# Projected states for block 0 as well: pairs (0,1), (2,3), (4,5), (6,7) in an attention and two-MLP kernel

## Chip, cores and metric

One Trainium2 (trn2) chip, of which the program uses one core. The metric is the device time of one execution in microseconds (us). All data are float32; the large products run in the engine's fp32r form, with every operand split into a high part and the rest, and three of the four partial products taken (`TERMS`).

## What is computed

For x of shape (8, 8, 512, 64) (batch, head, position, depth) and 32 states per batch and head, both attentions below are taken, the two results are joined along the positions, heads are laid side by side (512 columns), and the 4352 rows go through two MLPs.

```python
scores = scale * np.matmul(x, state.transpose(0, 1, 3, 2))      # softmax over the 32 states
xread = np.matmul(a, state)
scores2 = scale * np.matmul(state, x.transpose(0, 1, 3, 2))     # softmax over the 512 positions
sread = np.matmul(a2, x)
...
h = x @ w_in                                                     # 512 -> 2048, float64 weights in memory
g = np.maximum(h, 0.0) + alpha * np.minimum(h, 0.0)
y = g @ w_out                                                    # 2048 -> 512
...
h2 = y @ w2_in
out = (h2 - np.tanh(h2)) @ w2_out
```

The MLP weights lie in memory as 64-bit numbers; the kernel reads them as pairs of 32-bit words and makes float32 pairs of them itself.

## The kernel before

**Blocks and visits.** A block is one batch of 512 rows; block 8 holds the 256 rows of `sread`. The first MLP goes over the blocks; of each it makes 16 visits (block, f), f being one slice of 128 of the 2048 inner columns. The order of visits is written out: (0, 0..7), (1, 0..15), (0, 8..15), (2, 0..15), (3, ...) and so on. A visit issues, in this order: `emit_h` (L607), the first product into `ps_h`; the plan's "early" work; `act_a` (L621), the leaky slope on ScalarE and VectorE; "gap" and "mid" work; `emit_o` (L635) of the visit two before, 12 matmuls of the second product into four banks; `act_b`, the split of g; then "late" and "end" work and the stores. All engines run their own instructions in program order. What stands in "early", "gap" and so on is a timetable written by hand: `at(i, f, place, work)` from L1017 on. The second MLP follows (Strassen-like chunks and pairs) and is not touched.

**First product.** For blocks 1 to 7 the matrix that multiplies w_in is not `xread` but the attention matrix (two groups of four heads, `X[0, blk, g]`), and w_in is multiplied by the states beforehand: `project_one` (L401) takes three matmuls for quarter q (512 of the 2048 columns), group g and half p, and makes a high and a low part (ScalarE L415, VectorE L416). So h needs 2 x 3 = 6 matmuls. A projection serves two blocks at once: two blocks' states share the 128 columns of the product, and the halves that belong to the other block go through DRAM (`pw_dram`) and are read back by `load_parts` (L429). The pairs are (1,2), (3,4), (5,6), and 7 alone. `SN` holds the split states that a projection reads: `state_mask` (L348) and `state_turn` (L355) make them, with one VectorE operation each (L351, L371).

**Block 0** works otherwise: `spread` (L479) and `read` (L584) make `xread` itself, in four pieces of 128 rows (fp32 matmuls, then a split on ScalarE and VectorE, L338 and L339), and h takes 4 x 3 = 12 matmuls with the plain w_in (L614).

**Conversion of the weights.** 32 jobs, 16 for slices of w_in and 16 for slices of w_out, in the order of `jobs` (L128). A job's words come by one DMA of 512 KB into a ring of four `raw` tiles; then ScalarE takes the absolute value (`conv_a`), VectorE clamps and shifts (`conv_b`, L116 and L118), joins the sign (`conv_s`, L121), ScalarE and GpSimd make the high and low parts (`conv_c`, `conv_d`). A tick (`conv_step`, in two halves) moves every job in flight by one phase: tick t runs `conv_b` and `conv_s` of job t - 2 and `conv_d` of job t - 4, and loads job t + 1. The 36 ticks stand: 6 in the opening, two a visit in (0, 0..7), and 14 in (1, 0..13).

**Opening.** Before the first visit a list written by hand runs the attention of block 0 (`a` for the first four heads, `c` for the other four), with the ticks between its steps:

```python
for z in [a.spread, a.s0, a.s1, tick, a.s2, c.spread, a.s2t, c.s0, a.s3, c.s1, a.s3x, c.s2, c.s2t, c.s3,
          a.s4, c.s3x, tick, a.s4m, a.s4t, c.s4, tick, tick, c.s4m, c.s4t, a.r0, a.r1, tick,
          c.r0, c.r1, slopes, tick, load_next_x, load_next_x]:
    z()
```

**Queues.** Every DMA is issued by SP, in program order: an issue that must wait (a raw tile not yet free, a part not yet made) holds all that come behind it. After its use w_in is written to DRAM for block 8 (`save_w_in`, eight transfers of 1 MB, in (0, 9) to (0, 15) and (2, 1) to (2, 7)); the half sums of block 0's y are stored after (0, 7) and read back in (0, 10).

Of the kernel before, what the change touches and what calls it, by code (L numbers as in the profile page):

```python
# [35 lines left out]
def attention_and_two_mlps(ctx, tc, x, state, w1_in, w1_out, alpha, w2_in, w2_out, out):  # L36
# [32 lines left out]
    mask = const.tile([P, GH], F32, name="mask")  # L69
    par = const.tile([P, 2], F32, name="par")  # L70
# [30 lines left out]
    def raw_words(r, layer, f, half):  # L101
        if half == 0:
            wi = w1_in if layer == 0 else w2_in
            nc.sync.dma_start(
# [3 lines left out]
        else:  # L108
            wo = w1_out if layer == 0 else w2_out
            nc.sync.dma_start(out=r.rearrange("p e w -> p (e w)"), in_=wo[f * P:(f + 1) * P, :])  # L110
# [17 lines left out]
    jobs = [(0, 0)] + [j for f in range(1, NF // 2) for j in ((f, 0), (f - 1, 1))] + [(7, 1)]  # L128
# [216 lines left out]
    def lead(b):  # L345
        return b if b % 2 or b == B - 1 else b - 1
# [26 lines left out]
    def parts_tile(b, q, g):  # L373
        if b == 1 and q < 3:
            open_wo(NF // FQ - 1)
            t = WO[NF // FQ - 1][:, :, 2 * (q % 2) + g, :]
        else:
# [6 lines left out]
               for b in range(1, B) if b == lead(b) for q in range(NF // FQ) for g in range(NG)}  # L384

    def staged(b):


        if b > 1:
            return (work.tile([P, DM], F32R, tag="cm", name="ph", bufs=3),  # L390
                    work.tile([P, DM], F32R, tag="cq", name="pl", bufs=3))
        k = n_staged[0]
        n_staged[0] += 1
        if k < 4:
            open_wi(NF // FQ - 1)
            return tuple(WI[NF // FQ - 1][:, i, k % NCC, :] for i in range(2))
        return tuple(work.tile([P, DM], F32R, tag=t, name="pe", bufs=1) for t in (("e2", "e2t"), ("sc", "at"))[k % 2])

    n_staged = [0]

    def project_one(b, q, g, p):  # L401


        both = b + 1 < B
        cols, d = (slice(2 * p, 2 * p + 2), slice(0, P)) if both else (slice(3 * p, 3 * p + 1), slice(p * HP, (p + 1) * HP))
        ps = ps_a.tile([P, DM], F32, tag="a", name="ps_p")[:P if both else HP]
        for k, (i, j) in enumerate(TERMS):
            nc.tensor.matmul(ps, lhsT=SN[b, g][:, i, cols, :].rearrange("p k m -> p (k m)"),  # L408
                             rhs=WI[q][:, j, g * NP + p, :], start=(k == 0), stop=(k == 2))
        if b == 1 and p == 0:  # L410
            parts_tile(b, q, g)
            hi, lo = PW[b, q, g]
        else:
            hi, lo = staged(b)
        nc.scalar.copy(hi[d], ps)  # L415
        nc.vector.tensor_tensor(lo[d], ps, hi[d].bitcast(F32), op=ALU.subtract)  # L416
        if b == 1:

            e = slice((1 - p) * HP, (2 - p) * HP)
# [32 lines left out]
    def attention(b, g, spare=False):  # L452
# [26 lines left out]
        def spread():  # L479
            sn = work.tile([P, 2, NP, 2, D], F32, tag="sn", name="sn")[:, 0]  # L480
            nc.vector.tensor_tensor(
                sn.rearrange("p a q d -> p (a q) d"),
                SG[b, g].unsqueeze(1).to_broadcast([P, GH, D]),
                mask.unsqueeze(2).to_broadcast([P, GH, D]), op=ALU.mult)
            st["sn"] = sn

        def s0():
            if b == 0:
                ps = psum([P, S], "ps_st")
                for p in range(NP):  # L490
                    nc.tensor.transpose(ps[:, p * P:(p + 1) * P],
                                        st["sn"][:, p].rearrange("p q d -> p (q d)"), ident)
                stt = work.tile([P, NP, HP], F32, tag="stt", name="stt", bufs=4)
                for p in range(NP):
                    nc.scalar.copy(stt[:, p], ps[:, p * P + p * HP:p * P + (p + 1) * HP])
                STT[b, g] = stt
# [87 lines left out]
        def read(p):  # L584
            if b == 0:
                ps = ps_acc.tile([P, S], F32, tag="acc", name="ps_x")
            else:
                ps = psum([P, S], "ps_x")
            nc.tensor.matmul(ps, lhsT=st["sn"][:, p].rearrange("p q d -> p (q d)"), rhs=st["at"],
                             start=True, stop=True)  # L590
            split_x(0, b, g * NP + p, S, ps)

        def s6():
# [8 lines left out]
        steps = dict(spread=spread, s0=s0, s1=s1, s2=s2, s2t=s2t, s2b=s2b, s3=s3, s3x=s3x, s3b=s3b, s4=s4, s4m=s4m,  # L602
                     s4t=s4t, s4b=s4b, s5=s5, s6=s6, r0=partial(read, 0), r1=partial(read, 1))
# [753 lines left out]
```

## Time and profile before

| | |
|---|---|
| median of 3 runs | 1460.18 us (1459.79 to 1461.02) |
| the profiled execution's own time | 1461.7 us |
| its span, first to last instruction | 1459.9 us |
| mean granted TensorE clock | 0.985 of full speed |
| TensorE busy | 1399.3 us, 96% of the span |
| VectorE, ScalarE, GpSimd busy | 67%, 50%, 37% |

The profile is one execution. A page gives the sums of each engine and a strip of 40 equal slices; windows give the same sums for chosen stretches; groups give operations of one line with count, busy time (overlaps counted once) and mean duration; waits say which engine stood idle until which other had finished; the timeline gives instructions in order of time. TensorE is PE, VectorE DVE, ScalarE ACT, GpSimd POOL, SyncE SP there. Since matmuls overlap, the time that one costs is busy time over count and not the mean duration.

### The profile page before, as it was taken

What the parts mean: (1) busy time and instruction counts of PE and PEld (TensorE: products, weight loads), DVE (VectorE), ACT (ScalarE), POOL (GpSimd) and SP (SyncE); (2) the same over time, 40 slices, a digit from 0 to 9 for tenths busy, and PEclk for the clock granted to TensorE, in tenths of its full rate; (3) what the DMA queues carried; (4) which work ended last, traced back from release to release, by engine and by line L of the source; (5) the groups of instructions that cost most, each with busy time, mean ns of one, the idle gap of its engine ahead of it and who ended that gap; (6) DMA issues with size and microseconds to landing.
All of it is one profiled execution on the core that took longest, in us unless ns stands there. A gap on an engine that the chain in (4) does not pass through costs nothing.

```text
span 1459.9 us, 22884 instructions
## 1 busy us (share of the span) xinstructions
PE 1399.3 (96%) x8188; PEld 1190.5 (82%) x8188; DVE 972.6 (67%) x1430; ACT 730.7 (50%) x1322; POOL 538.8 (37%) x414
## 2 busy tenths in 40 slices
PE   5779999999999899999999999999999999999998
PEld 2557677777787777778987888888879999999998
DVE  7889756556767677765446646465357698777874
ACT  4666644444655555654334545454355354444443
POOL 3645400000455455446001221122025576666662
PEclk8989999999999999999999999999999999999999
DMA  6447438976777777679836774543978733444421
GB/s 164 137 140 197 129 136 286 314 248 173 217 209 222 210 241 209 219 232 312 258 102 254 256 251 157 211 176 141 346 263 313 257 105 128 145 138 138 145 81 37
DMA packets 227906, 288.12 MB, mean 197 GB/s; under 512 B 57808, under 2 KB 133584, under 8 KB 226768
## 3 DMA queue, kind: packets, MB, share of 16 engines
q1 hardware_dynamic: 227792, 286.66, 61.4%
q8 instruction: 64, 1.05, 0.3%
q14 instruction: 50, 0.41, 0.1%
HBM read 166.54 MB, written 117.96 MB: 195 GB/s over the span
## 4 chain that ended last, share of the span: by engine, by line
PE 61%; DMA 6%; DVE 6%; ACT 2%; issue 2%; POOL 1%; SPq 1%; ACTq 0%; DVEq 0%; POOLq 0%
PE ps_m L1027 21%; PE ps_m L837 17%; PE acc L645 12%; PE ps_h L617 6%; PE ps_m L911 2%; DMA gt<-g 1%; DMA pw<-pw 1%; DVE g L629 1%; DVE ps_h L624 1%; DMA c_raw<-in_moe_w_in 1%; PE ps_p L408 1%; DMA ch<-wc 1%; DMA g<-t 1%; ACT g L628 1%; DVE c_m L121 1%
## 5 line engine op out<-in xcount | busy, mean ns | idle before, releaser
L645 PE MATMUL acc<-g,wo 128*128 128x512 f32 (+1 forms) x1728 | 405.8, 384 | 2.8 <-ACT g L628 1.4
L645 PEld LDWEIGHTS acc<-g,wo 128*128 128x128 f32 x1728 | 311.8, 190 | 75.0 <-issue 6.5
L1027 PE MATMUL ps_m<-wp,s 128*128 128x256 f32 x2856 | 343.4, 283 | 1.4 <-ACT e L1010 1.4
L1027 PEld LDWEIGHTS ps_m<-wp,s 128*128 128x128 f32 x2856 | 342.9, 192 | 1.9 <-ACT e L1010 1.8
L837 PE MATMUL ps_m<-x,ch 128*128 128x512 f32 x1344 | 306.5, 390 | 2.9 <-ACT c L843 2.2
L837 PEld LDWEIGHTS ps_m<-x,ch 128*128 128x128 f32 x1344 | 251.9, 188 | 57.0 <-ACT c L843 3.4
L972 DVE TENSOR_TENSOR s<-gt,s 128x512 fp32r<-128x512 f32 (+1 forms) x216 | 214.4, 1043 | 46.7 <-ACT s L988 45.7
L629 DVE SCALAR_TENSOR_TENSOR g<-ps_h,sign,g 128x512 fp32r<-128x512 f32 (+1 forms) x144 | 103.5, 719 | 156.2 <-ACT g L628 155.9
L628 ACT ACTIVATE g<-ps_h,sign 128x512 fp32r<-128x512 f32 (+1 forms) x144 | 95.5, 663 | 174.2 <-PE acc L645 120.3
L988 ACT CAST s<-gt 128x512 fp32r<-128x512 f32 (+1 forms) x216 | 120.0, 596 | 80.9 <-PE ps_m L1027 39.0
L617 PE MATMUL ps_h<-x,pw 128*128 128x512 f32 x600 | 157.3, 397 | 3.0 <-DMA pw<-pw 2.4
L624 DVE SCALAR_TENSOR_TENSOR ps_h<-ps_h,sign,t 128x512 f32<-128x512 f32 (+1 forms) x144 | 104.4, 725 | 67.1 <-ACT t L623 66.3
L617 PEld LDWEIGHTS ps_h<-x,pw 128*128 128x128 f32 x600 | 110.0, 188 | 28.6 <-issue 3.2
L238 POOL TENSOR_TENSOR c_q<-c_m,c_q 128x512 int32<-128x512 int32 x32 | 41.3, 1291 | 242.2 <-DVE c_m L121 223.7
L850 POOL TENSOR_TENSOR t<-c,t 128x512 f32<-128x512 f32 x32 | 44.9, 1402 | 230.7 <-ACT t L847 225.8
L623 ACT ACTIVATE t<-ps_h,slope 128x512 f32<-128x512 f32 (+1 forms) x144 | 95.8, 665 | 54.3 <-PE ps_h L617 53.9
L859 DVE TENSOR_TENSOR c<-ps_m,c 128x512 f32<-128x512 f32 x96 | 65.7, 689 | 84.2 <-PE ps_m L837 71.8
L847 ACT ACTIVATE t<-c 128x512 f32<-128x512 f32 x96 | 60.6, 633 | 85.3 <-DVE c L859 73.6
L265 POOL TENSOR_TENSOR c_o<-c_q,c_o 128x512 fp32r<-128x512 f32 (+1 forms) x48 | 55.8, 1163 | 95.4 <-ACT c_o L263 95.4
L954 POOL TENSOR_TENSOR s<-gt,gt 128x512 f32<-128x512 f32 (+1 forms) x36 | 54.7, 1529 | 87.5 <-DMA gt<-g 86.6
L843 ACT COPY c<-ps_m 128x512 f32<-128x512 f32 x96 | 56.0, 586 | 51.1 <-PE ps_m L837 43.6
L168 POOL TENSOR_TENSOR cq<-cm,cq 128x512 int32<-128x512 int32 x32 | 42.5, 1329 | 95.2 <-DVE cm L121 68.4
(142 smaller groups left out, 1657.9 us busy)
## 6 DMA issues: line engine op xcount, KB each, us to landing
g<-t SPq DMA_DIRECT2D x128, 256.0 KB, 2.3
gt<-g SPq DMA_DIRECT2D x64, 512.0 KB, 4.8
wc<-c_o SPq DMA_DIRECT2D x112, 256.0 KB, 3.7
ch<-wc SPq DMA_DIRECT2D x56, 512.0 KB, 6.9
pw<-pw SPq DMA_DIRECT2D x96, 256.0 KB, 5.5
wp<-wc SPq DMA_DIRECT2D x28, 512.0 KB, 7.3
xr<-in_x SPq DMA_DIRECT2D x64, 128.0 KB, 3.1
raw<-in_moe_w_in SPq DMA_DIRECT2D x16, 512.0 KB, 3.9
```

The costliest lines, as they stand in the source:

```text
L617: nc.tensor.matmul(ps[:, :n], lhsT=w[i], rhs=xt[:, j, :n], start=(k == 0 and m == 0), stop=(k == len(pairs) - 1 and m == 2))
L623: nc.scalar.mul(t, ph, slope[:, f:f + 1])
L624: nc.vector.scalar_tensor_tensor(ph, ph, sign[:, f:f + 1], t, op0=ALU.mult, op1=ALU.max)
L628: nc.scalar.mul(g[:, 0, :n], ph, sign[:, f:f + 1])
L629: nc.vector.scalar_tensor_tensor(g[:, 1, :n], ph, sign[:, f:f + 1], g[:, 0, :n].bitcast(F32), op0=ALU.mult, op1=ALU.subtract)
L645: nc.tensor.matmul(acc[t][:, :n], lhsT=w[i][:, t * P:(t + 1) * P], rhs=g[:, j, :n], start=(first and k == 0), stop=(last and k == 2))
L837: nc.tensor.matmul(b, lhsT=w[p][:, cc], rhs=XT[key, i][cc][:, q], start=(i not in GOES_ON and cc == k == 0), stop=(cc == 1 and k == 2), sk ...
L847: nc.scalar.activation(t, h, AF.Tanh)
L859: nc.vector.tensor_tensor(h, ps[j, i], h, op=ALU.add)
L972: nc.vector.tensor_tensor(made[k - 1][:, 1], src, made[k - 1][:, 0].bitcast(F32), op=ALU.subtract)
L988: nc.scalar.copy(made[k][:, 0], source(blk, i, jj))
L1027: nc.tensor.matmul(dst[:, t * HW:(t + 1) * HW], lhsT=s[:, p, r, t * P:(t + 1) * P], rhs=w[:, q], start=first, stop=(jj == NJ // 2 - 1 and ...
```

## The change

Block 0 gets projected states too. The pairs become (0,1), (2,3), (4,5), (6,7), with the even block first; `spread` and `read` go, and h of block 0 takes 6 matmuls. The states of blocks 0 and 1 are masked and turned in the opening. Quarter 0 is projected at the end of the opening, quarter 1 in (0,2) and (0,3), quarters 2 and 3 in (1,4), (1,5), (1,9), (1,10). For quarters 0 and 1 a projection writes both parts to staging tiles, copies block 0's halves by DMA into the tile that h reads, and block 1's to DRAM; for all others everything goes through DRAM, and block 1 reads all its parts by `load_parts`. The jobs are reordered: four slices of w_in come first, (7, 0) is job 8, and w_out's slices 1 to 7 follow. The ticks stand: 8 in the opening, two a visit in (0, 0..3), one in (0, 4..7), 16 in (1, 0..13). Three loads of states and the first load of weights are issued by ScalarE's queue. The half sums are read into two spare `x` tiles instead of `raw` tiles.

```diff
-    jobs = [(0, 0)] + [j for f in range(1, NF // 2) for j in ((f, 0), (f - 1, 1))] + [(7, 1)]
+    jobs = [(0, 0), (1, 0), (2, 0), (3, 0), (4, 0), (0, 1), (5, 0), (6, 0), (7, 0)]
+    jobs += [(f, 1) for f in range(1, 8)]
...
-        raw_words(raws[k], 0, *jobs[k])
+        raw_words(raws[k], 0, *jobs[k], nc.sync if k else nc.scalar)
...
     def lead(b):
-        return b if b % 2 or b == B - 1 else b - 1
+        return b - b % 2
...
-        if b == 1 and q < 3:
+        if (b == 0 and q < 2) or (b == 1 and q < 3):
             open_wo(NF // FQ - 1)
             t = WO[NF // FQ - 1][:, :, 2 * (q % 2) + g, :]
...
+    def staged(b, q, g, p):
+        if b > 0:
             return (work.tile([P, DM], F32R, tag="cm", name="ph", bufs=3),
                     work.tile([P, DM], F32R, tag="cq", name="pl", bufs=3))
+        if q < 2:
             open_wi(NF // FQ - 1)
+            t = WI[NF // FQ - 1][:, :, 2 * g + p, :]
+        else:
+            if len(extra) < 2:
+                extra.append(xpool.tile([P, 2, S], F32R, tag="x", name=f"extra{len(extra)}"))
+            t = extra[p]
+        return t[:, 0], t[:, 1]
...
+        ps = ps_a.tile([P, DM], F32, tag="a", name="ps_p")
         for k, (i, j) in enumerate(TERMS):
+            nc.tensor.matmul(ps, lhsT=SN[b, g][:, i, 2 * p:2 * p + 2, :].rearrange("p k m -> p (k m)"),
                              rhs=WI[q][:, j, g * NP + p, :], start=(k == 0), stop=(k == 2))
+        hi, lo = staged(b, q, g, p)
+        nc.scalar.copy(hi, ps)
+        nc.vector.tensor_tensor(lo, ps, hi.bitcast(F32), op=ALU.subtract)
+        d, e = (slice(k * HP, (k + 1) * HP) for k in (p, 1 - p))
+        if b == 0 and q < 2:
+            if p == 0:
+                parts_tile(b, q, g)
+            for k, t in enumerate((hi, lo)):
+                nc.sync.dma_start(out=PW[b, q, g][k][d].bitcast(F32), in_=t[d].bitcast(F32))
             for k, t in enumerate((hi, lo)):
                 nc.sync.dma_start(out=pw_dram[b, q, g][p, k, e], in_=t[e].bitcast(F32))
             return
         for k, t in enumerate((hi, lo)):
+            nc.sync.dma_start(out=pw_dram[b, q, g][p, k], in_=t.bitcast(F32))
...
-        if 0 < blk < B:
+        if blk < B:
             col = slice(f % FQ * P, (f % FQ + 1) * P)
             pairs = [([PW[blk, f // FQ, g][i][:, col] for i in range(2)], X[0, blk, g]) for g in range(NG)]
...
+        load_state(0, 0)
+        for b, g in ((0, 1), (1, 0), (1, 1)):
+            load_state(b, g, queue=nc.scalar)
         load_next_x()
+        conv_load(0)
         load_next_x()
-        for k in range(4):
+        for k in range(1, 4):
             conv_load(k)
...
+        for z in [masks[0, 0], turned[0, 0], masks[0, 1], a.s0, turned[0, 1], masks[1, 0], masks[1, 1], tick, a.s1, tick,
+                  turned[1, 0], turned[1, 1], a.s2, tick, a.s2t, c.s0, a.s3, tick, c.s1, a.s3x, c.s2, c.s2t, tick, c.s3,
+                  a.s4, c.s3x, a.s4m, tick, a.s4t, c.s4, a.s4b, tick, c.s4m, c.s4t, c.s4b, tick, slopes]:
             z()
+        for g in range(NG):
+            for p in range(NP):
+                project_one(0, 0, g, p)
+        load_next_x()
+        load_next_x()
...
-        for f in (*range(10), 12, 13):
-            if f in (5, 12):
+        for f in range(14):
+            if f in (11, 12):
...
-        turns = [(0, 1, 0, (0, "mid"), (2, "early")), (0, 2, 0, (1, "late"), (2, "gap")),
-                 (0, 1, 1, (3, "mid"), (4, "early")), (0, 2, 1, (3, "late"), (4, "mid"))]
+        turns = [(1, 2, 0, (5, "late"), (7, "late")), (1, 2, 1, (8, "late"), (9, "late"))]
...
+        todo = [(0, q, g) for q in range(1, NF // FQ) for g in range(NG)] + [(2, q, g) for q in range(NF // FQ) for g in range(NG)]
+        todo += [(b, q, g) for b in (4, 6) for g in range(NG) for q in range(NF // FQ)]
+        places = [(0, 2), (0, 3), (1, 4), (1, 5), (1, 9), (1, 10), (1, 14), (1, 15)] + [(0, f) for f in range(8, 14)]
+        places += [(0, 15)] + [(2, f) for f in range(15)]
...
+        at(0, 5, "late", partial(load_parts, 1, 0))
+        at(1, 0, "early", partial(load_parts, 1, 1))
+        at(1, 6, "end", partial(load_parts, 1, 2))
+        at(1, 10, "end", partial(load_parts, 1, 3))
+        at(1, 13, "late", partial(load_parts, 0, 2))
+        at(0, 9, "early", partial(load_parts, 0, 3))
...
-        for f in range(NF // 2):
+        for f in range(NF // 4):
             halves(0, f, "late", "end")
```

## Rows read from the trace of the kernel before

**Rows 1.** Page: span, part 1 (busy us), part 2 (GB/s of 40 slices).

```profile
span 1459.9 us, 22884 instructions
...
PE 1399.3 (96%) x8188; PEld 1190.5 (82%) x8188; DVE 972.6 (67%) x1430; ACT 730.7 (50%) x1322; POOL 538.8 (37%) x414
...
GB/s 164 137 140 197 129 136 286 314 248 173 217 209 222 210 241 209 219 232 312 258 102 254 256 251 157 211 176 141 346 263 313 257 105 128 145 138 138 145 81 37
```

**Rows 2.** Windows A to F: busy us of each engine, clock, DMA share, GB/s.

```profile
0.00:30.80 30.80, 18.64 (x50) 9.02 (x51) 20.61 (x47) 13.84 (x27) 7.37 (x11) 0.83 0.59 159
30.80:108.67 77.87, 57.62 (x350) 42.15 (x349) 66.69 (x121) 49.35 (x97) 42.89 (x32) 0.89 0.51 144
108.67:181.92 73.25, 68.53 (x294) 54.16 (x293) 63.71 (x92) 46.63 (x85) 35.38 (x26) 0.97 0.59 162
181.92:195.57 13.65, 13.65 (x93) 11.02 (x92) 9.64 (x19) 5.55 (x11) 1.29 (x1) 1.00 0.00 1
195.57:253.56 57.99, 57.24 (x287) 45.93 (x286) 30.12 (x55) 24.80 (x43) 0.00 (x0) 1.00 0.73 256
253.56:350.38 96.82, 93.61 (x467) 70.25 (x466) 59.06 (x108) 46.04 (x83) 0.00 (x0) 0.98 0.82 254
```

**Rows 3.** VectorE's groups in stretch B: count, busy us, mean ns of one, idle before.

```profile
L118 DVE TENSOR_SCALAR cm<-cm 128x512 int32<-128x512 int32 x16 | 12.8, 798 | 0.5
L121 DVE SCALAR_TENSOR_TENSOR cm<-raw,cm 128x512 int32<-128x512 int32 x16 | 12.1, 753 | 0.2
L116 DVE TENSOR_SCALAR cm<-cm 128x512 f32<-128x512 f32 x16 | 8.3, 518 | 0.0
...
L351 DVE TENSOR_TENSOR sm<-sg,par 128x128 f32<-128x128 f32 x4 | 3.1, 776 | 0.0
...
L371 DVE TENSOR_TENSOR snp<-ps_st,snp 128x128 fp32r<-128x128 f32 x4 | 1.1, 284 | 1.0 <-ACT snp L370 1.0
```

**Rows 4.** VectorE's groups in stretch C.

```profile
L118 DVE TENSOR_SCALAR cm<-cm 128x512 int32<-128x512 int32 x13 | 16.2, 1249 | 0.4
L116 DVE TENSOR_SCALAR cm<-cm 128x512 f32<-128x512 f32 x13 | 10.9, 837 | 0.0
...
L121 DVE SCALAR_TENSOR_TENSOR cm<-raw,cm 128x512 int32<-128x512 int32 x13 | 9.3, 712 | 0.0
L416 DVE TENSOR_TENSOR wo<-ps_p,wo 128x512 fp32r<-128x512 f32 x4 | 2.7, 676 | 0.0
```

**Rows 5.** TensorE's groups in stretch E.

```profile
L617 PE MATMUL ps_h<-x,wi 128*128 128x512 f32 x84 | 20.5, 393 | 0.8 <-DVE g L629 0.8
L408 PE MATMUL ps_p<-wi,snp 128*128 128x512 f32 x49 | 13.9, 390 | 0.0
```

**Rows 6.** Timeline of stretch A: start us, duration us, engine, line, operation.

```profile
18.11 3.75 PE L589 MATMUL ps_x<-at,sn 128*128 128x512 f32 x4 [4.60 <-DVE at L560]
...
30.36 0.18 DVE L89 TENSOR_TENSOR slope<-alpha_sb,sign 128x16 f32<-128x16 f32 x1
...
30.80 0.69 ACT L623 ACTIVATE t<-ps_h,slope 128x512 f32<-128x512 f32 x1
```

**Rows 7.** Timeline of SP from 80 to 90 us.

```profile
84.00 1.18 SPq L421 DMA_DIRECT2D pw<-wi  x2
85.27 1.19 SPq L424 DMA_DIRECT2D wo<-wi  x2
```

**Rows 8.** DMA issues: KB of one, median us from issue to landing.

```profile
pw<-pw SPq DMA_DIRECT2D x96, 256.0 KB, 5.5
...
wo<-pe SPq DMA_DIRECT2D x4, 128.0 KB, 2.2
```

**Rows 9.** Windows of 5 us with full DMA engines.

```profile
10.00:15.00 5.00, 3.28 (x15) 1.49 (x14) 4.01 (x7) 1.54 (x4) 0.00 (x0) 1.00 1.03 343
275.00:280.00 5.00, 3.10 (x14) 1.92 (x13) 2.03 (x4) 1.51 (x4) 0.00 (x0) 1.00 1.02 265
```

**Rows 10.** Waits of the first 360 us: us in all, times, longest.

```profile
ACT g L628 <- PE acc L645: 58.0, 26, 3.6
...
PE ps_h L617 <- DMA wo<-pe: 1.8, 1, 1.8
```

More of the change, by code (lines that the diff above doesn't have):

```diff
@@ L68, in attention_and_two_mlps @@
     ident = const.tile([P, P], F32, name="ident")
-    mask = const.tile([P, GH], F32, name="mask")
-    par = const.tile([P, 2], F32, name="par")
+    par = const.tile([P, 16], F32, name="par")[:, :2]
     alpha_sb = const.tile([P, NF], F32, name="alpha_sb")
@@ L99, in w_out, with raw_words @@
         return WO[f // FQ][:, part, f % FQ, :]
-    def raw_words(r, layer, f, half):
+    def raw_words(r, layer, f, half, queue=nc.sync):
         if half == 0:
             wi = w1_in if layer == 0 else w2_in
-            nc.sync.dma_start(
+            queue.dma_start(
                 out=r.rearrange("p (c f) w -> p c (f w)", c=NCC),
@@ L109, in raw_words @@
             wo = w1_out if layer == 0 else w2_out
-            nc.sync.dma_start(out=r.rearrange("p e w -> p (e w)"), in_=wo[f * P:(f + 1) * P, :])
+            queue.dma_start(out=r.rearrange("p e w -> p (e w)"), in_=wo[f * P:(f + 1) * P, :])
     def high_abs(m, r):
@@ L309, in attention_and_two_mlps, with load_state @@
     xraw, SG = {}, {}
-    def load_state(b, g, tag="sg"):
+    def load_state(b, g, tag="sg", queue=nc.sync):
         sg = work.tile([P, D], F32, tag=tag, name=f"{tag}{b}_{g}", bufs=4)
-        nc.sync.dma_start(out=sg, in_=state[b, g * GH:(g + 1) * GH].rearrange("h n d -> (h n) d"))
+        queue.dma_start(out=sg, in_=state[b, g * GH:(g + 1) * GH].rearrange("h n d -> (h n) d"))
         SG[(b, g) if tag == "sg" else (b, g, 0)] = sg
     def load_x(b, g):
-        if b < 2:
-            load_state(b, g)
         if b == 0:
@@ L477, in transpose_pair @@
             st["xt", p] = xt
[L479 to L485, printed above, removed]
-        def s0():
[L488 to L496, printed above, removed]
+        def s0():
             transpose_pair(0)
@@ L582, in s5 @@
             st["wide"] = wide
[L584 to L591, printed above, removed]
         def s6():
@@ L612, in emit_h @@
         else:
-            w = [WS[f][:, i] if blk else w_in(f, i) for i in range(2)]
+            w = [WS[f][:, i] for i in range(2)]
             pairs = [([w[i][:, cc, :] for i in range(2)], X[0, blk, cc]) for cc in range(NCC)]
@@ L653, in load_half_sum @@
         for k in range(2):
-            t = work.tile([P, 2, S], F32, tag="raw", name="half", bufs=4)
+            t = extra[k].bitcast(F32)
             nc.sync.dma_start(out=t, in_=y_dram[0][2 * k:2 * k + 2].rearrange("c p n -> p c n"))
```

54 lines of the change are left out of this document (11 added, 43 removed).

## The prediction

> **What bounds the kernel now.** I read the page first. Of a span of 1459.9 us TensorE is busy for 1399.3 us, so all its idle time is some 60 us [rows 1]. The second view is the table of windows, cut where visits around the change begin; a visit is (block, f), and its mark is the ScalarE scaling of its h (act_a). I name the stretches A (start to the first act_a), B (visits (0,0) to (1,0)), C (to (1,13)), D (to (0,8)), E (to (2,0)) and F (to (3,0)) [rows 2]. The reader is to see two regimes. In A, B and C together TensorE is idle for 12.2 + 20.3 + 4.7 = 37 us, and VectorE is busy for 66.7 of 77.9 us in B and 63.7 of 73.25 in C: 130.4 of 151.1, a share of 0.863. There the conversion of the weights, which goes through VectorE, sets the pace. In D, E and F TensorE is idle for 0, 0.8 and 3.2 us: there each matmul taken away shortens the run, and VectorE has about half of its time free. Third, the groups of one engine inside B, C and E give the price of each operation [rows 3 to 5], and the timeline shows how A ends [rows 6].
>
> **The change, part by part.**
>
> Block 0's first product has 12 matmuls a visit now and 6 afterwards: 96 fewer, 48 in visits (0,0) to (0,7) and 48 in (0,8) to (0,15). In E 84 of them take 20.5 us, 0.244 each [rows 5]. The projections stay at 64 calls of 3 matmuls (four pairs in place of three pairs and a single block); only their places change. So the change does take about 23 us from TensorE; the question is how much of it lies where TensorE is the bound.
>
> Stretch A. Out go the two spreads, the mask, and the four reads; the reads' fp32 products for the first group of heads alone span 3.75 us of TensorE [rows 6], and their four splits leave VectorE. In come two splits of the attention matrix, four masks and four turns (two of each were made in B), two more conversion jobs (6 before the first act_a, 4 now), and four projections. A conversion job costs VectorE 0.80 + 0.75 + 0.52 = 2.07 us and a turn 0.28 [rows 3]; the low half of a projection, and a split of the same shape, 0.68 [rows 4]. A spread is 256 wide, between a turn (128) and a split (512), so I take 0.5. A mask shows 0.78 [rows 3]; most of the four run before the scores are there, where VectorE is idle (it is busy for 20.6 of 30.8 us [rows 2]), so between 0 and 3.1 I take 1.1. The list grows by 2 x 2.07 + 4 x 0.68 + 2 x 0.68 + 1.1 + 1.1 = 10.4 and loses 4 x 0.68 + 1.0 = 3.7: 6.7 us net. VectorE was done with the list, slopes last, at about 30.5 [rows 6]; so the last low half is ready at about 37.2.
>
> Then comes SP. Each projection issues four DMAs, two into the tile that the product reads and two to DRAM; two issues of this form took 1.19 us [rows 7]. So four projections hold SP for 9.5 us. The first low half is ready three halves earlier, at 35.2; twelve issues (7.1 us) stand from there to the last one that h needs, which lands some 2.2 us behind its issue [rows 8]: 44.5. With the last matmuls act_a comes at 45.0, 14.2 later than now. Bounds: 40 if SP were never late (37.2 + 2.2 + 0.6), 50 if raw words or projections come late in addition.
>
> In A three state loads and the first weight load move to ScalarE's queue. ScalarE is idle there, and SP is spared four issues of about 0.6 us. I book nothing for it: from 10 to 15 us the DMA engines are full already, at a share of 1.03 and 343 GB/s [rows 9]. The Trainium skill, "DMA: Bandwidth & Descriptors", Issuing engines are not separate DMA queues, says that DMAs from any engine run on the same 16 DMA engines, and that a second issuer saves issue time alone. By that rule the first act_a stays at 45.0; if issue time bounded the start, it would come 2.4 us sooner, at 42.6. No row here has a load issued by ScalarE, so the trace cannot yet decide.
>
> Block 1's x loads (eight issues, 4.8 us of SP) stand behind the projections' DMAs, and weight load 9 behind them, issued at about 51; its words are wanted in visit (0,1), and three jobs' words lie ready before it, which hides that; without them it would cost visit (0,1) some 4 us of landing.
>
> Stretches B and C. In B VectorE loses four jobs (12 instead of 16), 8.3 us, and four masks at 0.78 with four turns at 0.28, 4.2 us [rows 3]; projections are four before and after. 66.7 becomes 54.2. In C it gains two jobs, which cost more there (1.25 + 0.84 + 0.71 = 2.80 [rows 4]), 5.6; it loses four low halves, 2.7, and gains two masks, 1.6. 63.7 becomes 68.2. Together 122.4 us of VectorE work instead of 130.4. At the same busy share, 0.863, that is 141.8 us; TensorE's load falls by some 15 us, so fewer operations wait for it, and I take 0.88: 139.1. Two waits are new. H of (0,4) needs the second quarter's tile, whose last DMA is issued in the middle of (0,3). H of (1,12) needs parts that are stored in (1,10) and loaded behind that, one group of them only when a raw buffer comes free in (1,11); a load of this form lands in 5.5 us [rows 8] against some 4 us of cover. The like wait for a DMA is 1.8 us in the trace [rows 10]. Between 0 and 4 us for both, most of it under VectorE's own work: 1. Act_a of (1,13) comes at 45.0 + 139.1 + 1 = 185.1, where it is at 181.9: +3.2. Bounds for B and C: 131.6 (share 0.93) to 146.
>
> D gets four projections, 12 matmuls at 0.284 (13.9 us for 49 [rows 5]), +3.4; and h of (0,8) loses six, -1.5. D's DMA share is 0.00 now [rows 2], which covers the stores.
>
> E loses 42 matmuls in h, 10.2 us, and two projections, 1.7. But E moves 256 GB/s x 58 us = 14.8 MB now [rows 2]; with one more load of 1 MB and one visit's stores (1 MB) less it is the same in 46 us, 322 GB/s, where slices of the page reach 346 at most [rows 1]. When the engines were full, from 275 to 280, TensorE stood for 1.9 us [rows 9]. So +2, between 0 and +8. F loses two projections, -1.7; block 6 stores twice what block 7 did, 4 MB more in F, where 254 GB/s becomes about 300: booked at 0, up to +4. Behind F the diff leaves the work as it is.
>
> **Sum:** 3.2 + 3.4 - 1.5 - 10.2 - 1.7 + 2.0 - 1.7 = -6.5. The profiled execution took 1461.7 us, 1.5 over the median of the runs, 1460.18. 1461.7 - 6.5 = 1455.2 for an execution like it, 1453.7 for the median.
>
> **Rivals.**
>
> (a) The start is not given back, and the run gets slower. B and C are then set by the waits inside a visit (ScalarE waited 58.0 us for the second product over the first 360 us [rows 10]) and not by VectorE's amount. B falls by its four jobs alone, 8.3, C grows by 5.6 and the new waits by 2: (1,13) comes 14.2 - 8.3 + 5.6 + 2 = 13.5 late, and with D to F (-9.7) the sum is +3.8: 1464. It decides where (1,13) comes over 9.7 late, behind 191.6. For it: in B TensorE (57.6 of 77.9) and VectorE are both well used and neither is full. Against: both lose over 10 us there.
>
> (b) The transfers take E's gain. If spread over visits they go no faster than the present 256 GB/s, E stays near 54 instead of 48: +6 more, 1459.7, no measurable change. For it: the stall at 275 us. Against: D lies empty and takes 2 MB of the stores.
>
> (c) B and C get denser, since TensorE and VectorE are both relieved: at 0.93, 131.6 us, (1,13) comes 4.3 us early, and the sum is -14.0: 1446.2.
>
> **How the numbers follow.** Forecast 0.53 (1449 to 1457), (c) 0.15, (b) 0.17, (a) 0.15. A measurement of this kernel tells about 0.2%, 2.9 us, from no change. Faster is the forecast with (c), 0.68; the same is (b), 0.17; slower is (a), 0.15. The range, 1445 to 1463, leaves out the far parts of (a) and (c), some 0.17 together; it holds the bounds of A (-5 and +5, in part recovered in B) and of the DMA terms.
>
> **What would show it.** In the new profile: first act_a near 45, with SP issuing almost without a gap for 9 us before it and VectorE nearly idle for its last 6; act_a of (1,0) near 107, of (1,13) near 185; D near 15.5 and E near 48, with six h matmuls a visit; a DMA share over 0.9 through E. If the first act_a lies at 40 or 50, the step on SP or that on the raw words fails. If (1,13) comes behind 191, VectorE's amount was not the bound. If E is longer than 52 with TensorE idle, the transfers were under-priced. F shorter by more than 4 us, or the rest behind it moved, would be something that I have not seen.

## The result, and the profile after

The changed kernel is slower: 1468.84 us, median of 4 runs (1467.59 to 1469.69), against 1459.99 for the kernel before beside it (4 runs, 1457.52 to 1461.02). The ratio is 1.0062 [1.0045, 1.008]. The time lies above the whole predicted range.

The page of the changed kernel has the span and the busy times that answer to [rows 1]:

```profile
span 1467.8 us, 22725 instructions
...
PE 1382.1 (94%) x8084; PEld 1176.6 (80%) x8084; DVE 972.0 (66%) x1427; ACT 728.7 (50%) x1320; POOL 535.8 (37%) x414
```

TensorE does 17.2 us less, where the prediction had reckoned about 23, and the span is 7.9 us longer: TensorE now idles for 85.7 us instead of 60.6. The windows of the changed kernel, cut at the same marks as [rows 2] (A to F in order; columns as there), say where:

```profile
0.00:48.90 48.90, 18.10 (x47) 9.55 (x48) 31.51 (x60) 19.27 (x38) 15.23 (x17) 0.73 0.64 164
48.90:114.92 66.02, 49.20 (x304) 34.51 (x304) 52.38 (x97) 41.11 (x76) 31.81 (x24) 0.86 0.67 184
114.92:196.03 81.11, 68.36 (x277) 52.66 (x276) 64.96 (x91) 47.68 (x87) 37.88 (x30) 0.92 0.63 187
196.03:213.23 17.20, 16.64 (x104) 13.23 (x103) 12.63 (x26) 8.05 (x15) 1.29 (x1) 1.00 0.26 94
213.23:263.48 50.25, 47.99 (x241) 36.65 (x240) 30.46 (x59) 23.54 (x42) 0.00 (x0) 1.00 0.92 313
263.48:359.00 95.52, 91.86 (x468) 71.75 (x467) 57.90 (x108) 45.57 (x84) 0.00 (x0) 1.00 0.87 288
```

Length against before: A +18.1, B -11.85, C +7.9, D +3.55, E -7.7, F -1.3, and -0.7 behind F. (One slip of the prediction: its F ends at act_a of (2,15), not of (3,0). The last row here is cut at the same visit, so the difference stands.) The reader is to see two things. E and F did shrink, nearly as forecast. And act_a of (1,13) comes at 196.0, 14.1 late: the start lost 18.1 us and B and C gave back only 4 of them, although VectorE has 13 us less to do there (117.3 instead of 130.4). Its share in B and C fell to (52.38 + 64.96) / 147.13 = 0.80.

The waits of the changed kernel over its first 370 us (us in all, times, longest) name what TensorE now stands for:

```profile
ACT g L594 <- PE acc L611: 64.4, 29, 3.3
...
ACT t L589 <- PE ps_h L583: 39.5, 26, 8.2
...
PE ps_h L583 <- DMA wo<-pw: 6.0, 2, 5.4
PE ps_h L583 <- DMA pw<-pw: 4.7, 2, 3.1
...
PE ps_h L583 <- DMA wo<-wi: 3.7, 1, 3.7
...
PE ps_h L583 <- DMA xs<-xw: 2.0, 1, 2.0
```

L583 is the first product, L589 the changed kernel's act_a, L594 its act_b. Before, the first product waited for a DMA once, for 1.8 us [rows 10]; now four visits wait 16.4 us together. `wo<-wi` is the opening; `xs<-xw` is the wait of (0,4): the product reads the tile in `wo`, and the weight loads beside it wait for `wo<-wi`, so that the small load which the row names seems to have landed at about the same moment; `wo<-pw` is (1,8) and `pw<-pw` is (1,12). The first, from the timeline of the end of stretch A (start us, duration us):

```profile
35.65 2.75 SPq L414 DMA_DIRECT2D wo<-wi  x2
...
38.44 1.24 SPq L416 DMA_DIRECT2D pw<-wi  x2
39.79 1.18 SPq L414 DMA_DIRECT2D wo<-wi  x2
...
44.91 1.19 SPq L414 DMA_DIRECT2D wo<-wi  x2
46.15 1.23 SPq L416 DMA_DIRECT2D pw<-wi  x2
...
47.25 3.33 PE L583 MATMUL ps_h<-x,wo 128*128 128x512 f32 x7 [3.74 <-DMA wo<-wi]
...
47.89 2.39 PEld L583 LDWEIGHTS ps_h<-x,wo 128*128 128x128 f32 x6 [0.17 <-DMA wo<-wi]
48.90 0.69 ACT L589 ACTIVATE t<-ps_h,slope 128x512 f32<-128x512 f32 x1 [8.15 <-PE ps_h L583]
```

SP issues sixteen DMAs from 35.65 to 47.4, each pair into the tile followed by a pair to DRAM that nothing needs for 40 us. The last pair for the tile goes out at 44.91; the product can go on at 47.25, and its last weights (PEld) have landed at 47.89. The longest wait, from the timeline of (1,8):

```profile
147.88 4.18 SPq L426 DMA_DIRECT2D wo<-pw  x4
...
156.23 1.62 PE L583 MATMUL ps_h<-x,wo 128*128 128x512 f32 x3 [5.43 <-DMA wo<-pw]
...
160.02 0.69 ACT L589 ACTIVATE t<-ps_h,slope 128x512 f32<-128x512 f32 x1 [7.19 <-PE ps_h L583]
```

The load of block 1's parts for quarter 2 stands in (1,6) "end", but SP reaches it behind x loads, raw words and stores only at 147.88. The product stands from 150.80 on. The four transfers take 6.7 to 7.4 us each from issue to landing, so that the first two, one group of heads, are there 8.3 us after the first issue and the other two at 158.2.

### The profile page after: what moved, and what is told of

The parts are those of the page before. It is cut to its first block, busy times and chain, and to the rows that moved or that the text cites. A ratio compares the mean times of both kernels' runs of the same rounds, so it can differ in the third digit from the quotient of the medians.

```text
span 1467.8 us, 22725 instructions
## 1 busy us (share of the span) xinstructions
PE 1382.1 (94%) x8084; PEld 1176.6 (80%) x8084; DVE 972.0 (66%) x1427; ACT 728.7 (50%) x1320; POOL 535.8 (37%) x414
## 4 chain that ended last, share of the span: by engine, by line
PE 59%; DMA 7%; DVE 6%; ACT 2%; issue 2%; POOL 1%; SPq 1%; ACTq 0%; DVEq 0%; POOLq 0%
PE ps_m L993 20%; PE ps_m L803 17%; PE acc L611 12%; PE ps_h L583 6%; DMA gt<-g 1%; PE ps_m L877 1%; DMA pw<-pw 1%; DMA wp<-wc 1%; DVE ps_h L590 1%; DVE g L595 1%; PE ps_p L404 1%; DMA ch<-wc 1%; DMA c_raw<-in_moe_w_out 1%; ACT g L594 1%; DMA g<-t 1%
## 5 line engine op out<-in xcount | busy, mean ns | idle before, releaser
L594 ACT ACTIVATE g<-ps_h,sign 128x512 fp32r<-128x512 f32 (+1 forms) x144 | 95.5, 663 | 184.0 <-PE acc L611 129.1
L583 PE MATMUL ps_h<-x,pw 128*128 128x512 f32 x648 | 170.8, 398 | 12.5 <-DMA pw<-pw 8.0
L583 PEld LDWEIGHTS ps_h<-x,pw 128*128 128x128 f32 x648 | 118.7, 189 | 41.0 <-issue 9.8
L589 ACT ACTIVATE t<-ps_h,slope 128x512 f32<-128x512 f32 (+1 forms) x144 | 95.8, 665 | 65.9 <-PE ps_h L583 65.4
L813 ACT ACTIVATE t<-c 128x512 f32<-128x512 f32 x96 | 60.6, 632 | 85.6 <-DVE c L825 77.9
```

The costliest lines, as they stand in the source:

```text
L583: nc.tensor.matmul(ps[:, :n], lhsT=w[i], rhs=xt[:, j, :n], start=(k == 0 and m == 0), stop=(k == len(pairs) - 1 and m == 2))
L589: nc.scalar.mul(t, ph, slope[:, f:f + 1])
L594: nc.scalar.mul(g[:, 0, :n], ph, sign[:, f:f + 1])
L813: nc.scalar.activation(t, h, AF.Tanh)
```

## The experiments

**Theory 1**, formed from that trace: the loss is waits for DMAs, SP's order in A and the loads of parts in C. **Theory 2**: B and C are set neither by these nor by VectorE's amount, but by the rows of waits inside a visit, or by another engine. The first four runs were made on the changed kernel.

**Parts earlier in block 1.** Loads of quarters 2 and 3 split by group and moved up; block 1's double ticks and two x loads moved out of their way.

```diff
-        at(1, 6, "end", partial(load_parts, 1, 2))
-        at(1, 10, "end", partial(load_parts, 1, 3))
+        at(1, 5, "end", partial(load_parts, 1, 2, (0,)))
+        at(1, 6, "gap", partial(load_parts, 1, 2, (1,)))
+        at(1, 10, "early", partial(load_parts, 1, 3, (0,)))
+        at(1, 10, "end", partial(load_parts, 1, 3, (1,)))
...
-            if f in (11, 12):
+            if f in (9, 10):
...
-                    for j, f in (((1, 4), (1, 10)), ((0, 9), (0, 15)))[i] if i < 2 else ((i, 6), (i, 13)):
+                    for j, f in (((1, 7), (1, 13)), ((0, 9), (0, 15)))[i] if i < 2 else ((i, 6), (i, 13)):
```

> Block 1's parts of quarters 2 and 3 are loaded earlier (and the x loads that stand before them on SP later; the two double ticks move from (1,11), (1,12) to (1,9), (1,10), so that the raw tile is free). Theory 1, h of (1,8) and (1,12) waits for DMAs and the time is lost there: the two waits of TensorE, 5.9 and 4.7 us, go to under 1 us each, stretch C falls from 81.1 to about 72 us, and the run from 1468.8 to about 1460. Theory 2, VectorE's conversions set C anyway and the waits lie beside them: C stays within 2 us of 81, the run within 2 us of 1469.

1466.5 us in one run. Windows B and C of this kernel:

```profile
50.07:116.75 66.68, 50.94 (x304) 36.12 (x304) 52.18 (x97) 41.05 (x75) 31.75 (x24) 0.84 0.66 181
116.75:194.06 77.31, 68.47 (x281) 52.47 (x280) 63.21 (x91) 47.80 (x87) 38.13 (x29) 0.93 0.65 192
```

C loses 3.8 us of the 9 that theory 1 hoped for; (1,8) still waits 3.3, and VectorE's share in C is 0.82. Waits for parts remain, so this run does not say what C would be without them. A's opening is unedited here and yet ends at 50.07, 1.2 us later than in the changed kernel: so much do two equal openings differ.

**Tile first.** The opening's DMAs to DRAM are kept back until all that h reads are issued.

```diff
-                nc.sync.dma_start(out=pw_dram[b, q, g][p, k, e], in_=t[e].bitcast(F32))
+                held.append(partial(nc.sync.dma_start, out=pw_dram[b, q, g][p, k, e], in_=t[e].bitcast(F32)))
+            if (g, p) == (NG - 1, NP - 1):
+                while held:
+                    held.pop(0)()
```

> For quarters 0 and 1, SP issues the DMAs into the tile that h reads first and block 1's stores to DRAM behind them. Theory 1, SP's order sets the first h: six issues of 0.61 us fewer stand before it, the first act_a comes at 45.2 instead of 48.9, the wait before (0,4) shrinks from 2.0 to under 1 us, and the run gets 3 to 5 us shorter, 1464 to 1466. Theory 2, the next stretches are set by VectorE's work: the first act_a moves to 45.2, but B grows by as much and the run stays within 1 us of 1469.

1473.27 us in one run. Windows A and B, and a wait of this kernel:

```profile
0.00:45.28 45.28, 18.25 (x47) 10.03 (x48) 31.33 (x60) 19.36 (x39) 15.41 (x17) 0.77 0.62 161
45.28:116.32 71.04, 52.02 (x304) 36.75 (x304) 52.16 (x97) 41.12 (x75) 31.77 (x24) 0.81 0.68 181
```

```profile
ACT cm L110 <- DMA raw<-in_moe_w_out: 5.3, 1, 5.3
```

A shortens by 3.6 us, six issues at some 0.61: SP's order did set the end of A. But B grows by 5.0. The next weight load now stands behind the kept-back stores and x loads, and ScalarE waits 5.3 us for its words, the very "4 us of landing" that the prediction had called hidden. It was hidden only while the start was late. The total fits neither theory: the run is 4.4 us slower than the changed kernel, of which A and B hold 1.4; it is one run.

**Both edits together.**

> Both edits together. Theory 1: the gains add, A 45, B 65, C 72 us, the run at 1456 to 1458, that is 2 to 4 us under the kernel before. Theory 2: the run stays at 1466 to 1469.

1465.61 us (5 runs, 1464.08 to 1466.47), ratio 1.0040 [1.0024, 1.0057]. Windows B and C; A ends at 45.19:

```profile
45.19:114.05 68.86, 49.31 (x304) 34.51 (x304) 52.07 (x97) 41.13 (x76) 31.67 (x24) 0.88 0.69 186
114.05:193.95 79.90, 69.54 (x281) 53.10 (x280) 63.37 (x92) 47.73 (x87) 38.20 (x29) 0.91 0.64 186
```

The gains of A and C do not add up; the wait for raw words is still 4.4 us.

**All loads of the start issued by SP again.**

```diff
-        raw_words(raws[k], 0, *jobs[k], nc.sync if k else nc.scalar)
+        raw_words(raws[k], 0, *jobs[k])
...
-            load_state(b, g, queue=nc.scalar)
+            load_state(b, g)
```

> The changed kernel with all start loads issued by SP in the same order. If the DMA engines set the arrival of the words (issue time alone is saved by a second issuer): the first act_a stays at 48.9 within 0.5 us. If the issues set it: the fourteen issues of SP grow by four of 0.4 to 0.6 us and the first act_a comes 2 us later, near 51.

1469.67 us in one run; the first act_a comes at 50.5, between 0.4 and 1.6 later than in the two kernels that issue from ScalarE (the changed kernel and "parts earlier"). That lies nearer to the second forecast, 51, than to the first, 48.9 within 0.5, but with 1.2 us between equal openings it is not told apart from nothing. The front of A points the same way: SP begins to issue the row of raw words at 7.40 us in the changed kernel, 8.11 in "parts earlier" and 8.73 here, and ScalarE starts on the second slice's words at 12.10, 13.23 and 14.18. The Trainium skill, "DMA: Bandwidth & Descriptors", Issuing engines are not separate DMA queues, lets a second issuer save issue time alone; the runs agree as far as their scatter goes, since the 0.4 to 1.6 us that ScalarE's queue saved are no more than the issue time of the four loads, some 2.4 us.

**X later.** On top of both edits, block 1's x loads move out of the opening.

```diff
-        load_next_x()
-        load_next_x()
+        at(0, 1, "late", load_next_x)
+        at(0, 3, "late", load_next_x)
```

> Both edits of the third run, and block 1's x loads (eight issues on SP) moved from the end of the opening into visits (0,1) and (0,3). Theory 1, in the second and third runs the words of the next weight slice stood behind these issues and ScalarE waited 5.3 us for them: that wait goes, B falls from 68.9 to about 64, the run from 1465.6 to about 1461. Theory 2, a visit's other waits set B: B stays above 67.

1462.21 us in one run. No wait for raw words of w_out is left in the list, and B is still 67.65. So the waits that theory 1 names do not set B. The next four kernels add unused work to this one, each on one engine, in the eight visits of B:

```diff
+            nc.vector.tensor_reduce(par16[:, 8:9], X[0, 0, 0][:, 0, :].bitcast(F32), axis=AX.X, op=ALU.max)
...
+            nc.scalar.copy(extra[0][:, 0], src)
...
+            nc.gpsimd.tensor_tensor(extra[0][:, 1], src, src, op=ALU.add)
...
-        for k, (w, xt) in enumerate(pairs):
+        for k, (w, xt) in enumerate(pairs * 2 if blk == 0 and f < NF // 2 else pairs):
+            k %= len(pairs)
```

> The kernel of the run before it with one more VectorE operation of 0.67 us in each of the eight visits of B (its result is not used). If VectorE's amount sets B (as the prediction took it): B grows by 5.4 us. If chains of waits in a visit set it, so that VectorE's idle time takes the work: B grows by less than 2 us.

> The kernel of the run with the x loads moved, with one more ScalarE copy of 0.6 us in each of the eight visits of B (result not used). VectorE's 4.5 us cost B nothing. If ScalarE's program order is what sets a visit: B grows by 4 to 5 us from 67.7. If no single engine's amount sets it, but the row of waits from engine to engine: under 2 us.

> The same with one more GpSimd addition of 1.3 us in each of the eight visits. If GpSimd (half idle in B) sets nothing: B stays within 1 us of 67.7. If the ticks run through GpSimd and VectorE is slowed beside it: B grows by 3 to 10 us.

> The same kernel with the six matmuls of h issued twice in the eight visits of B, which puts the 48 matmuls back that the change takes away there. If TensorE's amount does not matter in B: B grows by under 3 us. If the 48 matmuls were a gain that was lost elsewhere: B grows by 48 x 0.244 = 11.7 us.

The window B of "x later", and then of the kernels with more on VectorE, on ScalarE, on GpSimd and on TensorE, in this order:

```profile
45.73:113.38 67.65, 51.70 (x304) 36.14 (x304) 51.63 (x97) 41.14 (x75) 31.45 (x24) 0.84 0.73 189
```

```profile
45.65:112.86 67.21, 50.82 (x304) 35.38 (x304) 56.06 (x103) 41.20 (x75) 31.50 (x24) 0.82 0.73 191
```

```profile
45.04:112.87 67.83, 50.74 (x304) 35.77 (x304) 51.28 (x95) 45.31 (x83) 31.75 (x24) 0.84 0.73 189
```

```profile
45.41:113.17 67.76, 49.36 (x304) 34.73 (x304) 55.97 (x97) 41.05 (x75) 40.26 (x31) 0.86 0.73 189
```

```profile
47.77:117.12 69.35, 58.54 (x346) 42.12 (x346) 52.46 (x97) 41.37 (x75) 31.73 (x24) 0.89 0.68 178
```

VectorE takes 4.4 us more work with B 0.4 shorter, ScalarE 4.2 more with B 0.2 longer, GpSimd 8.8 more with B 0.1 longer. Of the 48 more matmuls the row shows 42 in B (the first visit's lie in A); TensorE's busy time grows by 6.8 us, its clock being higher (0.89 for 0.84), and they cost B 1.7 and A 2.0. B differs by 0.7 between the changed kernel and "parts earlier", whose B is the same, so that 4 us would show. No engine's amount sets B. The totals, 1466.5, 1467.65, 1466.85 and 1466.86 us in one run each, are 4.3 to 5.4 us higher than that of "x later". C, unedited in all five, is 76.8 in "x later" and 79.1, 79.3, 79.3 and 77.7 in the four; it is 79.9 in "both edits together" with the same C, so this may be scatter, but that some of the added work was paid in C is not ruled out. The row of C in "x later":

```profile
113.38:190.18 76.80, 67.47 (x281) 51.60 (x280) 63.48 (x92) 47.81 (x88) 38.19 (x29) 0.96 0.67 193
```

What lies behind F, the same work in all of these kernels, takes 1105.8 to 1109.6 us in the five profiles, so single totals that differ by 3 us say little.

**Ticks back.** What does a job cost in B, then? On top of "x later", block 0's visits run two ticks each again, as before the change, and block 1 only twelve; quarters 2 and 3 are projected from (1,1), and their parts loaded from (1,4).

```diff
-        for f in range(14):
-            if f in (9, 10):
-                halves(1, f, "early", "gap", "mid", "end")
-            else:
-                halves(1, f, "gap", "end")
+        for f in (*range(9), 11, 12, 13):
+            halves(1, f, "gap", "end")
...
-        places = [(0, 2), (0, 3), (1, 4), (1, 5), (1, 9), (1, 10), (1, 14), (1, 15)] + [(0, f) for f in range(8, 14)]
+        places = [(0, 2), (0, 3), (1, 1), (1, 2), (1, 5), (1, 6), (1, 14), (1, 15)] + [(0, f) for f in range(8, 14)]
...
-        at(1, 5, "end", partial(load_parts, 1, 2, (0,)))
-        at(1, 6, "gap", partial(load_parts, 1, 2, (1,)))
-        at(1, 10, "early", partial(load_parts, 1, 3, (0,)))
-        at(1, 10, "end", partial(load_parts, 1, 3, (1,)))
+        at(1, 4, "late", partial(load_parts, 1, 2))
+        at(1, 8, "late", partial(load_parts, 1, 3))
...
-        for f in range(NF // 4):
+        for f in range(NF // 2):
             halves(0, f, "late", "end")
```

> The first kernel of this call with the conversion ticks back at two a visit in all of (0,0) to (0,7), 12 in block 1, and the projections of quarters 2 and 3 and their loads three to four visits earlier. If B's idle VectorE time takes work for nothing: B grows by less than 4 us for four more jobs (8.3 us of VectorE), C falls from 80 to about 70 with no wait for parts, and the run comes to about 1453. If VectorE sets B: B grows by 8, C falls by 11, the run comes to about 1458.

1460.83 us (10 runs, 1454.87 to 1465.7), ratio 0.9996 [0.998, 1.0012]. Windows B, C and E of this kernel:

```profile
45.58:121.15 75.57, 55.87 (x307) 38.28 (x307) 61.08 (x108) 47.80 (x88) 40.00 (x30) 0.81 0.66 179
121.15:186.56 65.41, 62.56 (x279) 49.86 (x278) 57.43 (x81) 41.08 (x76) 29.71 (x22) 1.00 0.75 216
203.87:254.95 51.08, 48.22 (x241) 36.67 (x240) 30.46 (x59) 23.54 (x43) 0.00 (x0) 1.00 0.91 308
```

Four jobs more in B cost 7.9 us, 2.0 each, and C is 11.4 shorter: just the 8 and 11 that the second forecast gave for "VectorE sets B". Yet VectorE is busy for only 0.81 of this B, and unused work on it had cost nothing. That a job lengthens the row of steps from engine to engine, and not one engine's list, would fit both; it is not shown. In C there are four jobs fewer, and the waits for parts are gone from the list: TensorE is busy for 62.6 of 65.4 us, 0.96, at the full clock. B and C together take 141.0.

**The second half alone.** On the kernel before: only (0,8) to (0,15) use projected states, paired with block 7; the opening stays as it was, and the attention matrix of block 0 is kept in DRAM.

```diff
     def lead(b):
-        return b if b % 2 or b == B - 1 else b - 1
+        return B - 1 if b == 0 else b if b % 2 else b - 1
...
+            if b == 0:
+                nc.sync.dma_start(out=at_dram[g], in_=at)
...
-        if 0 < blk < B:
+        if 0 < blk < B or blk == 0 and f >= NF // 2:
...
+        todo += [(7, q, g) for q in (2, 3) for g in range(NG)]
+        places += [(1, f) for f in range(10, 14)]
...
+        at(1, 13, "late", load_at)
+        at(1, 14, "early", partial(load_parts, 0, 2))
```

> The kernel before, with projected states for block 0 in its second half alone, visits (0,8) to (0,15): block 0's states share the projections of block 7 for quarters 2 and 3, which move from (2,12) to (2,15) and before to (1,10) to (1,13); the opening and the first eight visits stay as they were, the attention matrix goes through DRAM and comes back in (1,13). Theory 1, the change lost in the opening and in B and C, and its gain lies where TensorE is the bound: E gets 10 us shorter, C and D together at most 4 longer, and the run comes to 1450 to 1455, faster than both. Theory 2, the freed time in E is taken by the transfers (E at 256 GB/s now): E falls by less than 5 us and the run stays at 1457 to 1460.

1462.88 us (12 runs, 1455.48 to 1466.39), ratio 1.0011 [0.9997, 1.0025]. That is above both forecasts, though E's change is that of the second. C, D, E and F of this kernel, and a VectorE operation of visit (0,11) inside E:

```profile
108.70:186.91 78.21, 72.88 (x310) 57.23 (x310) 69.29 (x98) 49.76 (x92) 35.33 (x26) 0.98 0.65 186
186.91:205.77 18.86, 16.55 (x97) 12.77 (x96) 13.52 (x28) 8.12 (x17) 1.29 (x1) 0.91 0.58 172
205.77:259.02 53.25, 49.97 (x246) 39.27 (x245) 31.39 (x59) 25.20 (x45) 0.00 (x0) 0.97 0.88 299
259.02:349.62 90.60, 87.81 (x450) 66.88 (x449) 55.25 (x103) 42.12 (x76) 0.00 (x0) 1.00 0.83 258
```

```profile
228.74 0.72 DVE L520 STREAM_TRANSPOSE sc<-ps_s 128x512 f32<-128x512 f32 x1 [2.88 <-DMA y<-y]
```

E shrinks by 4.7 us, not by 10: VectorE waits 2.9 us for a store of block 1's y, with the saves of w_in and the stores of parts on the DMA engines. C and D, which take over the projections, grow by 10.2 and not by 4 at most; F, which loses them, shrinks by 6.2. (The profiled execution took 1458.1 us, 4.7 less than the median, so the windows do not show what makes the median long.)

**The saves moved.** The first four saves of w_in go from (0,9) to (0,15) into (1,12) to (1,15); added to the second half alone, to "ticks back", and to the kernel before as a control.

```diff
-            at(*((0, 9 + 2 * k) if k < 4 else (2, 2 * k - 7)), "end", partial(save_w_in, k // 2, k % 2))
+            at(*((1, 12 + k) if k < 4 else (2, 2 * k - 7)), "end", partial(save_w_in, k // 2, k % 2))
```

> The kernel with projected states in block 0's second half alone, and four of the eight saves of w_in (1 MB each) moved from (0,9), (0,11), (0,13), (0,15) to (1,12) to (1,15), where the DMA engines have room. If full DMA engines took E's gain: VectorE's wait of 2.9 us for the y stores and TensorE's 3 us of waits in E go, E falls from 53.3 to 50 or less, D does not grow, and the run falls by 3 to 4 us from 1462.9. If not: E stays at 53.

> The kernel with the ticks back in B and the parts loaded early, and the same four saves moved to (1,12) to (1,15). If full DMA engines cost E what it has over 48 us: E falls from 51.1 to 49 and the run from 1460.8 to about 1458, a little under the kernel before. If not: both stay.

> The kernel before with the four saves moved alone. TensorE is busy for 57.2 of E's 58.0 us there, so there is little to give back: E falls by at most 0.8 us and the run stays within 1.5 us of 1460.5. If it falls by more, the gain of the two runs with this edit is not the changed kernel's.

With the second half alone: 1457.78 us (12 runs, 1453.91 to 1461.28), ratio 0.9984 [0.9973, 0.9996]. With "ticks back": **1455.93 us (9 runs, 1453.35 to 1458.29), ratio 0.9973 [0.9963, 0.9983]**, better than both kernels. On the kernel before: 1460.60 us (10 runs, 1459.31 to 1463.48), ratio 1.0001 [0.9991, 1.0012]. D and E of the first:

```profile
186.67:207.18 20.51, 17.06 (x97) 12.71 (x96) 14.25 (x29) 8.13 (x18) 1.29 (x1) 0.92 0.94 317
207.18:256.88 49.70, 48.54 (x246) 37.98 (x245) 30.65 (x57) 25.06 (x44) 0.00 (x0) 1.00 0.85 276
```

A, B, C, D and E of the second:

```profile
0.00:45.02 45.02, 17.68 (x47) 9.42 (x48) 31.21 (x60) 19.27 (x39) 15.23 (x17) 0.75 0.63 162
45.02:120.33 75.31, 56.28 (x307) 38.57 (x307) 61.27 (x108) 47.87 (x88) 40.06 (x30) 0.79 0.66 180
120.33:185.73 65.40, 62.60 (x279) 49.87 (x278) 57.41 (x81) 41.05 (x77) 29.70 (x22) 1.00 0.78 232
185.73:203.04 17.31, 15.76 (x100) 12.48 (x99) 12.73 (x26) 8.07 (x16) 1.30 (x1) 1.00 0.66 231
203.04:251.52 48.48, 47.52 (x241) 36.91 (x240) 30.47 (x59) 23.66 (x43) 0.00 (x0) 1.00 0.87 282
```

E of the control:

```profile
194.70:252.70 58.00, 57.25 (x287) 45.93 (x286) 30.16 (x55) 24.82 (x44) 0.00 (x0) 1.00 0.61 201
```

The same move is worth nothing where TensorE has 57 us of work in E, and 3.6 and 2.6 us of E where it has 48: the transfers became E's limit only once the matmuls were gone. In the first, D, into which saves now fall, grows by 1.65 in return. The medians fall by more than E does, 5.1 and 4.9 us; the profiles do not locate the rest, since they differ by over 4 us behind F, where the kernels are alike (1106.8 and 1111.3 us in the first pair, 1111.8 and 1107.1 in the second).

## Why the prediction was wrong

The sum was -6.5 and the span grew by 7.9, 14.4 apart. By its own steps:

**B and C: the step that failed.** "At the same busy share, 0.863 ... I take 0.88: 139.1", and 1 for the two new waits. Measured: 147.1, 7.0 more than the 140.1. VectorE's work was reckoned too high rather than too low (117.3 against 122.4), so the share is what failed: it fell to 0.80, and the four probes show that B's length does not follow VectorE's amount, nor that of ScalarE or GpSimd. What sets B instead stays open: waits from engine to engine are what is left, and which of them is the longest at each moment was not settled. Rival (a)'s sign, ScalarE's wait for the second product (58.0 us [rows 10], 64.4 in the first 370), says little of B and C. Only 3.0 and 9.0 us of it lay in B and C before, 5.7 and 12.7 after; the rest lies outside them. The rows of C, before and after:

```profile
ACT g L628 <- PE acc L645: 9.0, 4, 3.6
```

```profile
ACT g L594 <- PE acc L611: 12.7, 8, 2.6
```

The new waits were mis-sized besides: (0,4) 2.0 and (1,12) 4.7, and (1,8) with 6.0 was not on the list, because only the place of its load in the timetable was looked at and not what SP had to issue ahead of it, nor how soon behind it the product comes.

C was also put into the wrong regime. TensorE was busy for 0.94 of it before, VectorE for 0.87 [rows 2]. The change took 17 matmuls out of C, but TensorE's busy time there stayed, 68.4 us for 68.5, and its idle time grew from 4.7 to 12.75, of which 10.7 are the waits of (1,8) and (1,12). Those waits were paid for twice, it seems: behind each of them TensorE ran at the lower of its two clock levels, 1.2 GHz. The windows are of the first wait, of the stretch behind it, and of the stretch behind the longer part of the second:

```profile
150.00:156.00 6.00, 0.80 (x4) 0.36 (x3) 4.48 (x6) 1.92 (x4) 4.02 (x4) 0.96 1.06 269
156.00:162.00 6.00, 5.25 (x12) 3.72 (x13) 1.22 (x3) 1.25 (x2) 1.14 (x1) 0.50 0.44 132
186.00:193.00 7.00, 5.39 (x13) 3.78 (x14) 5.18 (x8) 1.75 (x3) 3.17 (x3) 0.51 0.49 124
```

C's mean clock fell from 0.97 to 0.92. In "ticks back", without these waits, it is 1.00, and 279 matmuls take TensorE 62.6 us where 277 took 68.4; no run shows how much of that the clock alone is worth. At the forecast's share of 0.88, its VectorE work would have made B 61.6 and C 77.5; moving the loads brought C from 81.1 to 77.3, so that B, 4.4 too long, is the larger part of what is left.

**A: right in mechanism, 3.9 us mis-sized.** Of 48.9 against 45.0, 2.6 are VectorE's list (the first low half is there at 37.8, not 35.2). From there to the last landing it is 10.1 us, where 9.3 were booked for twelve issues and a landing, and the last matmuls take 1.0, where 0.5 was booked. SP's sixteen issues in a row, VectorE idle behind them and the 2.3 us of landing were there as written, and "tile first" takes off what the order of the issues cost. That weight load 9 is hidden holds only for a late start.

**D and E: 1.7 and 2.2 us mis-sized.** D takes 3.55 more and not 1.9; TensorE did 11 more matmuls in it, where I had reckoned 6. In E the matmuls went nearly as worked out (46 fewer, 48 reckoned); the price for the transfers, +2, came to 4.2 at a DMA share of 0.92. The saves runs show that cause: with four transfers of 1 MB moved out of "ticks back", E falls from 51.1 to 48.5, against a forecast of 48.

**F and the rest** were right: -1.3 for -1.7, and -0.7 for 0.

The misses are 3.9 + 7.0 + 1.65 + 2.2 + 0.4 = 15.15, less the 0.7 of the rest: the 14.4, within rounding. Rival (a) was the case that came: it put (1,13) at +13.5 and it came at +14.1. That it is so near is luck in part, for two misses cancel: A was 3.9 longer than it had, B 3.6 shorter. Its 1464 fell short of the measured time mainly by what D and E took beyond the forecast, 3.85. Rival (c), denser B and C, was wrong in sign: with a lighter TensorE the other engines' shares fell.

The fastest version, "ticks back" with the saves moved, comes near the forecast's numbers: (1,13) at 185.7 (forecast 185.1), B and C 140.7 (140.1), E 48.5 (48), the run 1455.9 (1453.7). That does not confirm the forecast. It is another timetable, with 16 jobs in B and four saves out of E, neither of which the sum had; VectorE's work in B and C is 118.7 us there and not 122.4, its share 0.84 and not 0.88; and 2.5 of the 5.7 us that this profile's span gains on the one before lie behind F, where the work is the same. It shows that the change can gain some 4 us once its timetable is rewritten; that the amounts agree with the sum is in part luck.

## What to carry to other kernels

An engine that is busy for 0.86 of a stretch need not be what sets it: where two engines are both well used and neither is full, put a little unused work on each in turn, and believe in a bound only where the stretch grows. For each load that a change adds, write down what its queue has to issue ahead of it at that moment, and order a burst of issues by who needs them first. And when matmuls leave a stretch, its transfers stay: move their bytes to where the DMA engines are idle, or they take the gain back.

## What was not expected of the hardware

- One addition a visit on GpSimd made VectorE's own operations longer: its busy time in B rose from 51.6 to 56.0 us with the same 97 instructions. The Trainium skill, "GPSIMD Engine Reference", 1. Specifications, says that the two share their SBUF interfaces; the rows agree that VectorE slows down, and B hid it.
- TensorE's mean granted clock in B falls from 0.89 [rows 2] to 0.86 with the change and to 0.79 in the fastest version, while TensorE is busy for about 0.75 of the stretch in all three. Between the levels of 1.2 and 2.4 GHz that is 22, 28 and 42% of the stretch at the lower one. In the fastest version TensorE's busy time there is 7 us longer than in the changed kernel for three matmuls more, and the run is faster none the less.
- Loads of 256 KB that land in 5.5 us as a rule [rows 8] took 6.7 to 7.4 us each in (1,8), where the DMA engines were at a share of 0.93 (146 to 160 us); SP took 4.18 us to issue the four.
- "Ticks back" scatters from 1454.9 to 1465.7 over ten runs, where the kernel before beside it stays between 1459.3 and 1462.1; why was not found.
